# Another order of issue for a fused delta-rule attention and softplus MLP

## The chip, the cores and the metric

The kernel runs on one core of a Trainium2 chip. The metric is the device time of one execution in microseconds; lower is better. The core has a matrix engine (TensorE, PE in the profile, with the loading of its weights shown apart as PEld), three engines for elementwise work (VectorE = DVE, ScalarE = ACT, GpSimd = POOL) and SyncE (SP), which here only issues DMAs. Each of them works through a queue of its own in the order in which the instructions were written, and waits on semaphores for the others.

## The reference

Inputs are q, k, v and g of shape (4, 8, 768, 48), beta of shape (4, 8, 768), and two weights, `w_in` (384 x 2048) and `w_out` (2048 x 384). A gated delta rule runs over the 768 tokens, for 4 x 8 heads of width 48:

```python
k_n = k / (np.linalg.norm(k, axis=-1, keepdims=True) + 1e-06)
for t in range(S):
    readout = np.einsum('bhd,bhde->bhe', q[:, :, t], state)
    y[:, :, t] = g[:, :, t] * readout
    v_old = np.einsum('bhde,bhd->bhe', state, kt)
    state = state + bt[:, :, :, None] * np.einsum('bhd,bhe->bhde', kt, vt - v_old)
```

Its output, seen as 3072 tokens of 384 features, goes through an MLP: `h = x @ w_in`, then softplus, `max(h, 0) + log1p(exp(-|h|))`, then `@ w_out`. The output is 3072 x 384 in float32.

## The kernel before, in words

**Tiling.** The 768 tokens are cut into 12 chunks of 64. A chunk has 64 tokens of each of 4 x 8 heads, that is 256 tokens of the MLP. Within a chunk the recurrence over tokens is written as a triangular system. Its matrix is made from products of the normalized keys, and inverted by block elimination. What one chunk hands to the next is the state alone, 48 x 48 for each head.

**Stages.** For each chunk there are these steps, and their names are used below:

- *Norms*: the keys are squared, summed (`red`, L413), and a root is taken: on ScalarE for the first four chunks, on GpSimd as a power for the others (L427). Two small VectorE steps follow (L435, L437).
- *Front*: keys and queries are cast or scaled to 16 bits (`kn` L509, `qn`), transposed by TensorE against an identity matrix (L461, L526) and copied out of PSUM (`kqt`, L222 on ScalarE and L224 on the other two). The keys of chunks 8 to 11 and the queries of chunks 10 and 11 are turned by transposing DMAs instead (L444). Gram products follow (L598), with scaled copies of them (`kk`, L222 or L226) and masked ones (`mt`, L580).
- *Inverse*, for the groups of chunks 0, 1, (2, 3), (4, 5), ... (10, 11): 15 elimination steps, each a product and a sum (L717, L724; the first is L709), which stand on VectorE or GpSimd; then copies and small matmuls which make `td` and `z`.
- *Chain*, the part that is serial from chunk to chunk: products with the old state (L914), w (L947 for chunk 0, L953 for the others), u1 and u2 (L967, L980), the state's product (`smm`, L996) and its sum (`s`, L1010), the output's product (L1022) and the gate (`yg`, L1036, two instructions for a chunk). The output is turned by transposing DMAs for chunks 5 to 10 (L1046), and by TensorE (L1062) with a copy (`xt`) for the others.
- *Dense*, the MLP: `w_in` products (`h`, L1088), softplus (`ga`, L1100), `w_out` products (`o`, L1115), a copy out of PSUM (`osb`) and the stores (L1139). Chunks 0, 1, 10 and 11 have windows of their own, and the others go in pairs.

**What sets the order.** Every step of every chunk is an item with a number: `Program.add` records what it does, which engines may do it and what it depends on. Nothing runs in the order in which the items are recorded. A table of words in text, `_ORDER`, lists them: the letter is the engine (P, D, A, G, S for PE, VectorE, ScalarE, GpSimd, SyncE), the number the item's, and `Program.emit` issues them word by word. An item may only stand behind all that it depends on. The place in the table thus sets the order in each engine's queue, and the letter the engine where an item allows several. Buffers come from rings, such as 12 slots for f32 inputs (`r_f`), 5 PSUM banks (`p_d`) for attention, 2 (`p_h`) for h and 1 (`p_o`) for o. An item's buffer takes the first free slot when its first user is issued, and gives it back with its last, so the order in the table also decides which slot a tile gets and whom it waits for:

```python
for word in table.split():
    en, no = word[0], int(word[1:])
    it = self.items[no]
    for b in it.bufs:
        if b.ap is None:
            b.slot = b.ring.free.pop(0)
    it.fn(en)
```

The weights come by DMA from GpSimd's queue, `w_in` and `w_out` in four pieces each, and all else from SyncE's. Ninety-six items are "fills": one matmul of the identity with itself, 128 x 512, into a slot of `h` that nobody reads. The table decides how many of them are issued:

```python
def fill(en, hp=hp):
    nc.tensor.matmul(hp.ap, ident, ident[:, None, :].broadcast_to([P, 4, P]))
```

Of the kernel before, what the change touches and what calls it, by code (L numbers as in the profile page):

```python
# [1170 lines left out]
G0 D6 S22 D329 S23 D267 P213 D13 A234 A1 D16 S31 D14 P18 D19 D241 P242 G238 D235 S17 S33 P239  # L1171
A243 P255 A236 D240 D237 D264 P252 A256 A257 A253 A254 D265 D266 G268 D269 D270 S32 D9 G308 S25
A8 D271 D272 A311 D273 D274 A7 S40 D275 G276 G277 G278 P20 P312 A4 A15 G279 S41 S24 A304 A2 A313
A12 A21 P309 A310 P314 P317 D244 G280 A10 P245 D305 S34 S50 G281 D5 D318 S49 A319 A11 A3 G282
A306 G283 A316 A248 D315 D307 A366 D327 P249 P220 A250 P224 A251 G131 G284 D326 D328 A391 A247
S51 S52 P323 P207 D330 P159 G331 D367 G332 A368 D392 P320 S27 S43 A246 D324 G333 P186 A377 D369
D322 A288 D285 A393 P378 A290 P228 D394 P261 P173 A289 P146 D325 A380 A286 D321 G334 D291 D263
A379 P295 A287 G395 G370 D262 S26 G335 P258 D292 A296 S42 A297 D260 P396 P163 D259 G130 D294
D336 G337 P209 D397 A293 S59 G410 A373 P298 A299 P371 S58 G338 G339 D372 D809 G411 A300 P374
A376 G133 P301 D810 A302 P168 P403 A375 D404 A303 D406 A405 P811 P398 P175 D812 D340 S29 S28 S30  # L1180
P139 A813 A456 P814 D402 A400 G132 D407 A816 D815 D457 D401 G341 A808 G342 P386 P820 S61 D399
A387 D821 A388 G343 P381 D822 G134 D344 P823 P196 G345 A382 D824 D383 G346 P1027 D389 D408 D390
A351 G458 G135 D385 A349 D409 S60 A463 D352 A1028 D412 A347 G136 P1021 D413 A1022 D384 A350 D414
G415 D353 P1023 G416 P464 A348 D354 D459 G417 S70 A1024 P1025 P817 A818 P1033 S35 S36 P357 G418
S69 A819 A1026 D358 D460 P826 D825 A465 A359 D356 G419 A355 P1035 P461 A1034 G137 G420 P1029
D828 D827 P360 D467 A1036 P1044 A362 A462 P829 D361 D421 A1030 P1031 D422 P830 A832 D423 D466
G424 A1032 D831 P1045 D425 G426 S68 P363 S67 A364 P468 D365 P833 P1046 A481 G427 P1047 D469 A834
D835 P476 A1048 A477 D482 S38 G428 P839 S39 S37 A470 D431 D480 A478 D479 S45 A429 P1037 D840
D841 P471 P836 A473 P1038 A432 D433 P842 P1039 G590 D837 D838 G483 A430 A843 D475 D434 D484 P844
A472 P438 A439 A440 D436 P1040 P1053 A437 S44 S77 G500 D845 P447 S76 G485 A1054 D474 P441 P1061  # L1190
A442 D435 D846 P486 S86 G546 A443 P848 A449 A448 D487 P1057 A850 S85 A1062 P444 P493 G501 A571
S47 D547 D446 A445 A849 P1065 D495 P847 A1058 D497 D496 P851 A852 G548 P1051 D494 A1066 A1041
D572 D853 G573 P488 D492 S46 S78 A489 A1052 D490 D549 P1055 D498 D499 G502 P450 S48 P1059 A1056
G503 P857 A452 G504 G505 A451 S79 A1060 G506 P854 G507 D491 D855 G508 G509 G510 G511 P1067 S104
G512 S53 S87 S54 P1063 P1068 D856 D859 D574 P862 P1069 A1064 P453 S88 A553 D864 A557 D863 P866
D858 D867 A454 D575 P1070 A868 S103 A455 P865 P869 A1071 P558 A660 A871 A559 S55 S56 P1074 S57
# [76 lines left out]
```

## Time and profile before

| | |
|---|---|
| median of 3 runs | 239.28 us (238.65 to 243.46) |
| profiled execution | 239.09 us |
| its span | 237.3 us |
| mean granted TensorE clock | 0.984 |
| PE busy | 206.0 us (87%) |
| VectorE, ScalarE, GpSimd busy | 162.8, 155.8, 115.3 us |
| DMA | 30.30 MB, mean 128 GB/s |

All times in the profile are of one profiled execution. The span is what lies between its first and last instruction, and 1.8 us of its 239.09 lie around the span. In rows that group instructions there stand the line, the engine, the operation, the output and inputs by name, their shapes and a count; behind the first bar the busy time in us and the mean of one in ns; behind the second the time for which the engine was idle just before them, with the instruction whose end ended that. PE's busy time counts pipelined matmuls and runs from the start of the first to the modelled end of the last, so it tells of work at hand and not of peak speed.

### The profile page before, as it was taken

To read this page: it belongs to the slowest core of one execution; us is meant where nothing else is said; L and a number is where in the kernel's file an instruction comes from. 1 tells how busy PE (TensorE), PEld (TensorE's weight loads), DVE (VectorE), ACT (ScalarE), POOL (GpSimd) and SP (SyncE) were. 2 spreads that over 40 slices of the span, in tenths; PEclk is the share of its full clock that TensorE was granted. 3 is DMA by queue.
4 is the path that set the end of the run, shared out by engine and by line. 5 is a ranking of instruction groups with operands and counts; after the bars stand their busy time and mean duration, and the time that the engine had idled before them with its cause. 6 is when DMAs were issued, how large, how long until landed. Compare 5 with 4: busy or idle time off the path is not lost.

```text
span 237.3 us, 11021 instructions
## 1 busy us (share of the span) xinstructions
PE 206.0 (87%) x4787; PEld 130.4 (55%) x4787; DVE 162.8 (69%) x371; ACT 155.8 (66%) x332; POOL 115.3 (49%) x223
## 2 busy tenths in 40 slices
PE   4837865977987999989599999889999999999992
PEld 3723543754665665556355556455555555667761
DVE  7898994989978899995689768966648043521000
ACT  4999893955886789957189886348663766035520
POOL 5248989576767888988864763104721000000000
PEclk9999995999999999999999999999999999999999
DMA  6999999999899188789399676888635301242222
GB/s 117 179 196 171 194 205 210 185 146 188 151 181 149 37 150 153 204 134 151 86 162 154 119 143 77 130 174 155 116 89 115 69 7 33 64 92 50 53 50 66
DMA packets 101136, 30.30 MB, mean 128 GB/s; under 512 B 91808, under 2 KB 101056, under 8 KB 101088
## 3 DMA queue, kind: packets, MB, share of 16 engines
q1 hardware_dynamic: 96128, 24.96, 61.6%
q0 software_dynamic: 3712, 3.15, 9.3%
q10 hardware_dynamic: 1248, 1.49, 2.6%
q8 instruction: 37, 0.61, 1.1%
q14 instruction: 11, 0.09, 0.2%
HBM read 25.26 MB, written 4.72 MB: 126 GB/s over the span
## 4 chain that ended last, share of the span: by engine, by line
PE 63%; DVE 9%; issue 6%; ACT 6%; POOL 6%; DMA 5%; SPq 3%; DVEq 0%; ACTq 0%; POOLq 0%
PE h L1088 22%; PE o L1115 20%; PE d L598 3%; PE d L914 3%; PE d L1115 2%; SPq L345 2%; POOL tt L724 2%; DMA kqt<-kn 2%; POOL tmp L717 2%; PE d L1022 2%; DMA f<-in_k_dram 2%; ACT kk L222 2%; DMA f<-in_g_dram 2%; PE d L980 1%; DVE mt L580 1%
## 5 line engine op out<-in xcount | busy, mean ns | idle before, releaser
L1088 PE MATMUL h<-xt,w_in 128*128 128x512 f16 (+1 forms) x384 | 74.0, 330 | 0.3 <-DVE xt L224 0.2
L1100 ACT ACTIVATE ga<-h 128x512 f16<-128x512 f32 x96 | 56.5, 601 | 26.1 <-PE h L1088 21.2
L1115 PE MATMUL o<-w_out,ga 128*128 128x384 f16 x352 | 66.1, 327 | 0.0
L1115 PEld LDWEIGHTS <-ga 128*128 128x128 f16 x384 | 35.1, 98 | 22.3
L1088 PEld LDWEIGHTS <-w_in 128*128 128x128 f16 x384 | 35.1, 99 | 20.9 <-issue 0.7
L717 POOL TENSOR_TENSOR tmp<-nn,tt 128x56 f32<-128x56 f32 (+13 forms) x78 | 29.6, 379 | 19.9 <-DVE tt L724 12.1
L724 POOL TENSOR_TENSOR tt<-tt,tmp 128x56 f32<-128x56 f32 (+13 forms) x78 | 29.0, 372 | 6.1
L222 ACT ACTIVATE osb<-o 128x384 f32<-128x384 f32 x17 | 8.4, 492 | 25.1 <-PE o L1115 20.8
L427 POOL TENSOR_TENSOR nv<-nv,half_c 128x16 f32<-128x16 f32 x8 | 23.5, 2937 | 2.0 <-DVE nv L413 1.8
L580 DVE TENSOR_TENSOR mt<-d,mask 128x256 f16<-128x256 f32 x48 | 18.6, 410 | 4.8 <-ACT kk L222 2.2
L598 PE MATMUL d<-kqt 48*64 48x128 f16 (+1 forms) x448 | 11.4, 228 | 8.1 <-ACT kqt L222 4.6
L224 DVE CAST u<-d 128x384 f16<-128x384 f32 x21 | 11.4, 552 | 10.1 <-PE d L967 5.5
L1036 DVE TENSOR_TENSOR yg<-d,f 128x384 f16<-128x384 f32 x24 | 12.5, 546 | 8.4 <-ACT ga L1100 4.5
L222 ACT ACTIVATE u<-d 128x384 f16<-128x384 f32 x27 | 12.8, 494 | 6.0 <-PE d L980 3.2
L598 PEld LDWEIGHTS <-kqt 48*64 48x64 f16 x448 | 8.1, 118 | 14.8 <-issue 8.6
L222 ACT ACTIVATE kqt<-d 128x512 f16<-128x512 f16 (+1 forms) x23 | 14.1, 636 | 1.8 <-DVE w L953 0.8
L222 ACT ACTIVATE kk<-d 128x256 f16<-128x256 f32 x33 | 11.8, 385 | 4.9 <-PE d L598 3.1
L1010 DVE TENSOR_TENSOR s<-s,d 128x384 f16<-128x384 f16 x20 | 10.3, 542 | 5.8 <-PE d L996 5.4
L953 DVE TENSOR_TENSOR w<-f,d 128x384 f16<-128x384 f32 x22 | 11.5, 547 | 2.8 <-PE d L914 1.6
L413 DVE TENSOR_REDUCE nv<-f 128x16 f32<-128x768 f32 x12 | 11.2, 942 | 0.5 <-ACT f L402 0.5
L914 PEld LDWEIGHTS <-kqt 48*64 48x64 f16 x704 | 7.8, 108 | 6.2 <-issue 6.2
L914 PE MATMUL d<-s,kqt 48*64 48x48 f16 x704 | 9.7, 188 | 0.8 <-DVE qn L224 0.5
(134 smaller groups left out, 334.4 us busy)
## 6 DMA issues: line engine op xcount, KB each, us to landing
f<-in_k_dram SPq DMA_DIRECT2D x24, 192.0 KB, 7.5
f<-in_q_dram SPq DMA_DIRECT2D x24, 192.0 KB, 4.9
f<-in_v_dram SPq DMA_DIRECT2D x24, 192.0 KB, 4.7
out_dram<-osb SPq DMA_DIRECT2D x33, 96.0 KB, 3.4
f<-in_g_dram SPq DMA_DIRECT2D x24, 96.0 KB, 3.4
f<-in_g_dram SPq DMA_DIRECT2D x12, 192.0 KB, 5.6
w_in<-in_moe_w_in_dram POOLq DMA_DIRECT2D x4, 384.0 KB, 7.6
w_out<-in_moe_w_out_dram POOLq DMA_DIRECT2D x4, 384.0 KB, 8.9
```

The source lines that it names most:

```text
L222: nc.scalar.activation(o, x, AF.Copy, scale=float(sign))
L427: nc.gpsimd.tensor_tensor(nvs(), nvs(), half_c[:, :NU], ALU.pow)
L580: nc.vector.tensor_tensor(mt[c][p].ap[:, NP * g : NP * g + NP], bank(gb, p, n), mask[:, None, :].broadcast_to([P, NP, C]), ALU.mult)
L598: nc.tensor.matmul(o, kq(c, r, NP * g + i, FEAT[p], 0, C), x)
L717: ENG[en].tensor_tensor(t, nn.ap[:, :nb, j : j + 1, j + 1 :].broadcast_to([P, nb, w, n]), tt.ap[:, :nb, :w, j : j + 1].broadcast_to([P, nb ...
L724: ENG[en].tensor_tensor(rows, rows, t, ALU.add)
L914: nc.tensor.matmul(where(r, p)[:, h], kq(c, r, h, FEAT[p], off, off + C), s0[r].ap[FEAT[p], h], **start(h),)
L953: lambda en, p=p: nc.vector.tensor_tensor(w1[p].ap, vf.ap[:, p], hd(wp[p].ap), ALU.subtract),
L1036: lambda en, a=a: nc.vector.tensor_tensor(yg.ap[:, a], hd(yp[a].ap), gf.ap[:, a], ALU.mult),
L1088: nc.tensor.matmul(hp.ap[:, n * b : n * b + n], w_in[:, j, f * P : (f + 1) * P], xt.ap[:, j, t0 : t0 + n], start=(j == 0), stop=(j == 2),)
L1100: lambda en, hp=hp, o=gb: nc.scalar.activation(o.ap, hp.ap, AF.Softplus),
L1115: nc.tensor.matmul(op.ap[:, :DM], b.ap[:, col + c0 : col + c0 + 128], w_out[:, f, :], start=(f == 0), stop=(f == NF - 1),)
```

## The change

Only the table changes: `Program`, all items and their functions are the same letter for letter. The new table lists the same items in another order, and without the fifteen fills that the old one issues at its beginning. It has 1286 words where the old one has 1301. Of the 1286 items that both have, 212 stand on another engine: 60 go from ScalarE to VectorE and 56 from VectorE to ScalarE, 30 from VectorE to GpSimd and 29 back, 9 from ScalarE to GpSimd and 2 back; 14 DMAs go from SyncE's queue to ScalarE's and 12 back. The items per engine go from 320 to 323 on VectorE, from 327 to 318 on ScalarE, from 126 to 134 on GpSimd and from 160 to 158 on SyncE. The pieces of the weights come in another order: `w_in` pieces 1, 0, 3, 2 and then `w_out` 0 to 3 before; `w_in` 2, 3, 1, `w_out` 2, 1, 0, `w_in` 0, `w_out` 3 now. Each line of the table differs; the diff's first and last lines show the kind:

```diff
 _ORDER = """
-G0 D6 S22 D329 S23 D267 P213 D13 A234 A1 D16 S31 D14 P18 D19 D241 P242 G238 D235 S17 S33 P239
-A243 P255 A236 D240 D237 D264 P252 A256 A257 A253 A254 D265 D266 G268 D269 D270 S32 D9 G308 S25
...
+P1370 A1342 S1343 D1372 A1371 A1373 S1374
 """
```

What this makes of the queues is seen at three places. In these rows a name's number is that of the buffer.

VectorE up to chunk 0's gate (`yg`, L1036). `mt` are masked Gram products of later chunks, `kk` scaled ones, `tmp` and `tt` an elimination step, `nv` sums of squared keys, `u` chunk 0's. Before:

```order
L580 TENSOR_TENSOR mt_112<-d_176,mask 128x256
L224 CAST u_138<-d_174 128x384
L717 TENSOR_TENSOR tmp_120<-nn_118,tt_121 128x63
L724 TENSOR_TENSOR tt_121<-tt_121,tmp_120 128x9x7
L580 TENSOR_TENSOR mt_113<-d_176,mask 128x256
L580 TENSOR_TENSOR mt_113<-d_172,mask 128x256
L224 CAST u_141<-d_174 128x384
L413 TENSOR_REDUCE nv_98<-f_81 128x16
L580 TENSOR_TENSOR mt_112<-d_173,mask 128x256
L226 TENSOR_SCALAR kk_103<-d_173 128x4x64
L1036 TENSOR_TENSOR yg_148<-d_175,f_79 128x384
L1036 TENSOR_TENSOR yg_148<-d_174,f_79 128x384
```

The same place in the changed kernel:

```order
L724 TENSOR_TENSOR tt_121<-tt_121,tmp_120 128x12x4
L580 TENSOR_TENSOR mt_111<-d_176,mask 128x256
L717 TENSOR_TENSOR tmp_120<-nn_118,tt_121 128x39
L724 TENSOR_TENSOR tt_121<-tt_121,tmp_120 128x13x3
L717 TENSOR_TENSOR tmp_120<-nn_118,tt_121 128x28
L724 TENSOR_TENSOR tt_121<-tt_121,tmp_120 128x14x2
L413 TENSOR_REDUCE nv_97<-f_83 128x16
L580 TENSOR_TENSOR mt_110<-d_173,mask 128x256
L1036 TENSOR_TENSOR yg_148<-d_174,f_78 128x384
L717 TENSOR_TENSOR tmp_120<-nn_118,tt_121 128x15
L724 TENSOR_TENSOR tt_121<-tt_121,tmp_120 128x15
L1036 TENSOR_TENSOR yg_148<-d_175,f_78 128x384
```

Seven elimination steps of chunk 1 (steps 6 and 7 and the last five) now stand on VectorE ahead of chunk 0's second `yg`, and the last of them between its two; the copies of u stand on ScalarE or farther ahead. From chunk 0's first w (L947) to its second `yg` there are 15 rows in between before and 31 now.

SyncE around the transposing DMA of chunk 11's keys (`kqt`, L444). The gates g come in three pieces, one of L345 and two of L337; `f_78` holds chunk 8's gate, `f_82` chunk 9's, and the rows with `out_0_dram` are stores. Before:

```order
L444 DMA_TRANSPOSE kqt2_106<-kn3_92 128x8x128
L337 DMA f1_78<-in_g_dram 64x8x48
L1139 DMA out_0_dram<-osb0_168 64x384 x2
L345 DMA f1_78<-in_g_dram 64x16x48
L1139 DMA out_0_dram<-osb2_170 64x384
L345 DMA f5_82<-in_g_dram 64x16x48
L1139 DMA out_0_dram<-osb2_170 64x384
L337 DMA f5_82<-in_g_dram 64x8x48
L345 DMA f4_81<-in_v_dram 64x16x48 x2
L345 DMA f7_84<-in_v_dram 64x16x48
L337 DMA f5_82<-in_g_dram 64x8x48
L337 DMA f1_78<-in_g_dram 64x8x48
```

In the changed kernel the keys of chunk 10 are the second row and those of chunk 11 the sixth, `xt` is the output of chunks 6 and 7 as the MLP reads it, and chunk 8's gate is in slot `f_84`:

```order
L444 DMA_TRANSPOSE kqt2_106<-qn1_94 128x8x128
L444 DMA_TRANSPOSE kqt2_106<-kn3_92 128x8x128
L1046 DMA_TRANSPOSE xt1_151<-yg0_148 128x3x128
L1139 DMA out_0_dram<-osb2_170 64x384
L444 DMA_TRANSPOSE kqt3_107<-qn0_93 128x8x128
L444 DMA_TRANSPOSE kqt3_107<-kn2_91 128x8x128
L1139 DMA out_0_dram<-osb2_170 64x384
L1046 DMA_TRANSPOSE xt1_151<-yg1_149 128x3x128 x2
L1046 DMA_TRANSPOSE xt1_151<-yg0_148 128x3x128
L345 DMA f7_84<-in_g_dram 64x16x48
L345 DMA f4_81<-in_v_dram 64x16x48 x2
L345 DMA f6_83<-in_v_dram 64x16x48
```

One piece of chunk 8's gate still stands behind the key transposes, and its two others stand ahead of all four of them; the outputs of chunks 6 and 7 are now turned among them.

PE's first rows, as a difference (L287 makes beta, L526 transposes keys):

```order
-L1268 UNCONDITIONAL_BRANCH
-L1149 LDWEIGHTS ident
-L1149 MATMUL h_177<-ident 128x512
+L1267 UNCONDITIONAL_BRANCH
 L287 MATMUL d_172<-w_out 128x32 x4
 L526 LDWEIGHTS kn_89
```

The fills at the start of the queue are gone; PE has 9546 rows before and 9516 now.

More of the change, by code (lines that the diff above doesn't have):

```diff
@@ L1177 @@
[L1177 to L1182, printed above, removed]
@@ L1243 @@
+P1355 A1356 P1353 P1327 A1354 A1328 A1304 P1367 S1305 P1357 A1358 P1361 S1306 P1375 A1362 P1365
+S1320 P1323 A1324 P1376 P1377 P1368 A1366 P1329 P1331 A1330 P1378 P1337 P1333 D1379 S1299 A1380
+P1344 A1334 P1345 P1338 A1332 S1381 P1346 P1347 P1339 P1340 S1312 D1341 A1348 A1350 S1349 P1369
+P1370 A1342 S1343 D1372 A1371 A1373 S1374
 """
```

131 lines of the change are left out of this document (67 added, 64 removed).

## The prediction

> **What bounds the kernel now.** I read the page's totals first, then busy time by stretch, then the waits of VectorE, then the chain.
>
> ```profile
> span 237.3 us, 11021 instructions
> PE 206.0 (87%) x4787; PEld 130.4 (55%) x4787; DVE 162.8 (69%) x371; ACT 155.8 (66%) x332; POOL 115.3 (49%) x223
> PEclk9999995999999999999999999999999999999999
> ```
>
> No single engine fills the span, so the stretches decide. Columns: the stretch, its length, then busy time (and count) of PE, weight loads, DVE, ACT, POOL, then granted clock, DMA share and GB/s.
>
> ```profile
> 0.00:40.00 40.00, 25.20 (x485) 17.23 (x486) 33.61 (x106) 32.63 (x71) 26.75 (x67) 0.94 1.15 181
> 40.00:80.00 40.00, 33.83 (x945) 24.17 (x945) 35.36 (x74) 28.23 (x63) 28.24 (x43) 0.97 1.07 161
> 80.00:100.00 20.00, 19.98 (x551) 12.13 (x549) 19.25 (x37) 18.49 (x40) 17.88 (x30) 1.00 0.71 141
> 100.00:120.00 20.00, 15.99 (x490) 10.16 (x488) 14.80 (x30) 10.35 (x23) 17.19 (x35) 1.00 0.77 129
> 120.00:145.00 25.00, 25.00 (x668) 13.79 (x665) 19.56 (x47) 20.93 (x46) 13.67 (x26) 1.00 0.79 138
> 145.00:170.00 25.00, 22.91 (x571) 13.05 (x570) 18.95 (x40) 14.15 (x32) 8.25 (x17) 1.00 0.83 142
> 170.00:220.00 50.00, 50.00 (x994) 30.82 (x993) 19.84 (x40) 26.03 (x54) 3.32 (x10) 1.00 0.29 64
> 220.00:237.30 17.30, 13.14 (x95) 9.05 (x93) 1.47 (x3) 5.03 (x10) 0.00 (x0) 0.98 0.24 58
> ```
>
> PE is idle for 14.80 + 6.17 = 21.0 us in the first 80 us, for 4.0 us from 100 to 120, for 2.1 us from 145 to 170, and for 4.2 us at the very end, behind the last matmul. Elsewhere it has no gap: from 80 us on the kernel is bound by PE with two leaks, 6.1 us together. Ahead of 80 us VectorE is the fullest engine, 33.61 + 35.36 = 69.0 of 80 us, and it hardly waits. Its largest two waits between 6 and 80 us (engine, what waited, for whom; us, times, longest) are these:
>
> ```profile
> DVE xt L224 <- PE d L1062: 2.9, 1, 2.9
> DVE tmp L717 <- POOL tt L724: 1.0, 1, 1.0
> ```
>
> So the early stretch is a VectorE queue in order, fed just in time. The chain names the leaks (start, length, what):
>
> ```profile
> 36.62 2.11 issue
> ...
> 105.32 0.96 issue
> ...
> 113.10 2.56 issue
> ...
> 150.77 4.28 DMA kqt<-kn
> ...
> 162.92 3.73 DMA f<-in_g_dram
> ```
>
> "issue" is PE standing still inside a run of matmuls while it waits for nothing that the profile shows: 2.11 us in the transposes of chunk 0's y (which is also the 2.9 us above), 0.96 and 2.56 us in the leak from 100 to 120. The leak from 145 to 170 is SyncE's: the transposing DMA of chunk 11's keys, and then chunk 8's gate, which lands late.
>
> **The change part by part.** PE's matmuls are the same but for the fills, so a gain can only come out of the 31 idle microseconds, and a loss only adds to them.
>
> *VectorE up to chunk 0's y.* Between its first w (L947) and its second yg (L1036) VectorE has 15 rows before and 31 now. The prices (columns: group, count; busy, mean ns; idle before it and whose end ended that):
>
> ```profile
> L580 DVE TENSOR_TENSOR mt<-d,mask 128x256 f16<-128x256 f32 x48 | 18.6, 410 | 4.8 <-ACT kk L222 2.2 <-PE d L598 1.6 <-ACT ta L738 0.9
> L724 DVE TENSOR_TENSOR tt<-tt,tmp 128x39 f32<-128x39 f32 (+13 forms) x20 | 4.8, 239 | 0.7
> L717 DVE TENSOR_TENSOR tmp<-nn,tt 128x39 f32<-128x39 f32 (+13 forms) x20 | 4.7, 236 | 3.1 <-POOL tt L724 2.8
> L509 DVE TENSOR_TENSOR kn<-f,nv 128x768 f16<-128x768 f32 x5 | 5.0, 993 | 0.0
> L224 DVE CAST z<-d 128x256 f16<-128x256 f32 x11 | 4.4, 418 | 6.5 <-PE d L877 6.5
> L437 DVE RECIPROCAL nv<-nv 128x16 f32<-128x16 f32 x10 | 2.4, 237 | 0.1
> L435 DVE TENSOR_SCALAR nv<-nv 128x32 f32<-128x32 f32 (+1 forms) x4 | 0.8, 212 | 0.0
> L690 DVE COPY tt<-beta_p 128x32 f32<-128x32 f32 x2 | 0.7, 356 | 0.0
> L226 DVE TENSOR_SCALAR kk<-d 128x256 f16<-128x256 f32 x15 | 6.1, 411 | 0.6 <-PE d L598 0.5
> L224 DVE CAST u<-d 128x384 f16<-128x384 f32 x21 | 11.4, 552 | 10.1 <-PE d L967 5.5 <-PE d L980 4.4
> L224 DVE COPY kqt<-d 128x1024 f16<-128x1024 f16 (+1 forms) x7 | 4.5, 647 | 0.8 <-PE d L526 0.8
> ```
>
> Added: six elimination steps of two instructions (6 x 0.475 = 2.85), two masks (0.82), the norms' two small ones (0.45), a diagonal (0.36), one key scaling (0.99), two z (0.84): 6.31. Removed: two L226 (0.82) and two u (1.10): 1.92. Net 4.4 us. Ahead of that w the changed queue is shorter: four masks (1.64) and two steps (0.95) fewer, one copy of kqt more (0.65), the small rest about even: 1.9 less. Together +2.5 us for the second yg; instructions overlap a little, but VectorE has no wait there that could absorb it. Bounds: 0, if the ordering ends waits on PE that these rows stand beside, and 4.4, if the shorter head only waits for data. Between chunk 0's y and chunk 1's state product (L996) the changed order has less VectorE work (99 items ahead of that product, 104 before), between chunks 1 and 2 more (139 against 129), so I carry about +3 us to 80 us, with bounds 0 and 4.4; from there PE hands it on.
>
> *The leaks after 100 us.* In the changed SyncE queue the gate loads g8 stand, but for one piece, ahead of the key transposes of chunks 8 to 11; the loads of k, q, v, g for chunks 4 to 9 stand far ahead of their readers, where before several stood next to them. The 2.1 us from 145 to 170 goes. Of the 4.0 us from 100 to 120, 0.96 + 2.56 = 3.5 us is "issue", which no row ties to a queue that moves; I let it stay and take 0.5 us. Gain 2.6 us; bounds 0 (a later transfer is late instead) and 6.1.
>
> *The fills.* Fifteen matmuls whose product nobody reads go:
>
> ```profile
> L1149 PE MATMUL h<-ident 128*128 128x512 f16 x15 | 6.9, 520 | 3.0 <-DVE ident L206 3.0
> ...
> 23.05 1.06 PE L461 MATMUL d<-ident,qn 128*128 128x128 f16 x8
> ...
> 26.24 0.61 PE L526 MATMUL d<-ident,kn 128*128 128x128 f16 x8
> ```
>
> Their 6.9 us lie in PE's idle time, so nothing is gained but what stood in someone's way, 0 to 1 us. What they may buy is the clock: eight transposes take 1.06 us at 23 us and 0.61 us at 26 us. Without fills the three groups of transposes between 26 and 36 us could cost 0.45 us more each, 1.35 us, and the first matmuls of dense work at half speed a little more; VectorE's queue covers most of it. Cost 0.5 us, bounds -1 and +3. [...]
>
> *What moves between engines.* 212 of 1286 items change their engine; the counts per engine hardly change (VectorE 320 to 323, ScalarE 327 to 318, GpSimd 126 to 134). Which of them count is in the term above; from 170 us on neither engine matters, since PE is busy for 50.00 of 50 us.
>
> Sum: +3.0 - 2.6 + 0.5 = +0.9 us on a span of 237.3. The profiled execution took 239.09 us, 1.8 us around its span and 0.2 below the median of 239.28. Forecast 240 us.
>
> **The rivals.** *Faster: both leaks close and the early cost is hidden.* The wait of 2.9 us behind chunk 0's y need not recur, and with transfers issued early the "issue" stops, which fall where DMA is crowded (share 1.15 in the first 40 us, 0.77 from 100 to 120), may go with them. For it: after 80 us PE has always work when data is there. Against: nothing shows what "issue" waits for. Time: 239.1 - 6.1 = 233.0, and 231 if the 2.11 us goes too.
>
> *Slower: GpSimd's added work holds VectorE up.* Up to chunk 4's state product GpSimd takes on three more casts, four more tx copies, chunk 1's scaling of v and several clears, all beside the fullest engine.
>
> ```profile
> 29.85 1.12 DVE L947 TENSOR_TENSOR w<-f,nv 128x384 f16<-128x384 f32 x2
> 30.00 0.56 POOL L717 TENSOR_TENSOR tmp<-nn,tt 128x63 f32<-128x63 f32 x1
> 31.22 0.31 POOL L717 TENSOR_TENSOR tmp<-nn,tt 128x64 f32<-128x64 f32 x1
> L509 POOL TENSOR_TENSOR kn<-f,nv 128x768 f16<-128x768 f32 x5 | 7.4, 1484 | 4.6 <-PE d L996 3.4 <-DVE nv L437 1.2
> ```
>
> A GpSimd step of 0.31 us took 0.56 us beside a VectorE instruction that reads two SBUF tensors. If the stall goes the other way too, four full-size GpSimd instructions (1.484 us each, 5.9 us) stand against VectorE, and they come on top of the 4.4 us bound: 239.1 + 4.4 + 5.9 - 2.6 = 246.8 at worst; with half of the 5.9 us, 243.9. It decides once VectorE is busy for over 73 of the first 80 us instead of 69. Against it: before, GpSimd was busy for 55 of those 80 us without a wait of VectorE on it beyond 1.0 us. [...]
>
> *The change does nothing here.* If PE's total sets the end, only its idle time counts, and the new order closes one leak where it opens another: 238 to 240. That is the forecast's own middle.
>
> **How the numbers follow.** Forecast (small terms that cancel): 0.50. Faster rival: 0.26. Slower rival: 0.24. Some 2% of 239.3 us is what the runs shown can tell from no change (they spread from 238.65 to 243.46), so faster means below 234.5 and slower above 244.1. The forecast's own range from its terms: all at their good end 239.1 + 0 - 6.1 - 1 = 232.0, all at their bad end 239.1 + 4.4 + 3 = 246.5; half of each side, 235.5 to 243, holds most of it. The range to give has the faster rival in it and the slower one at its worst nearly: 232 to 246.5. The faster rival's 0.26 lies below 234.5 nearly whole, and the forecast's lower end adds 0.02: 0.28. Of the slower rival's 0.24 half lies above 244.1, and the forecast's upper end, where the clock or a new wait costs all of its bound, adds 0.10: 0.22. Within 2%: 0.50.
>
> **What would show it.** VectorE runs chunk 0's two yg back to back:
>
> ```profile
> 35.17 1.01 DVE L1036 TENSOR_TENSOR yg<-d,f 128x384 f16<-128x384 f32 x2
> ```
>
> They end at 36.2 us now; right if the second ends at 37 to 41. Leaks: PE's idle time from 145 to 170 us falls under 1 us, and the chain no longer holds a wait on in_g there; wrong if a DMA of a y (L1046) or a v replaces it. Fills: eight transposes (L461, L526) still at over 1 us after 26 us, and PE at full clock by 50 us. Faster rival: no "issue" piece over 1 us. Slower rival: VectorE instructions between SBUF tensors (L717, L947, L1010) with longer means than now. The forecast is wrong as a whole if PE's idle time in the first 80 us moves by over 5 us either way.

## The result and the profile after

The changed kernel takes 249.07 us (median of 4 runs, 248.34 to 250.93) beside 238.97 us for the kernel before on the same chip (4 runs, 237.76 to 243.46): a ratio of 1.045, 95% interval 1.037 to 1.054. It is slower, and its time lies above the range given. Ratios leave disturbed runs out, so they can differ a little from the quotient of two medians. The profiled execution took 248.88 us with a span of 247.2, 9.9 us more than before.

The page's totals of the changed kernel:

```profile
span 247.2 us, 11000 instructions
PE 208.1 (84%) x4772; PEld 133.1 (54%) x4772; DVE 166.1 (67%) x381; ACT 152.6 (62%) x319; POOL 119.7 (48%) x224
```

Busy time by stretch of the changed kernel, with the stretches and columns of the prediction:

```profile
0.00:40.00 40.00, 20.45 (x384) 16.35 (x385) 34.53 (x104) 25.36 (x51) 27.88 (x68) 1.00 1.14 179
40.00:80.00 40.00, 31.63 (x882) 22.25 (x884) 33.16 (x77) 27.43 (x59) 29.72 (x39) 0.96 1.08 180
80.00:100.00 20.00, 17.19 (x489) 11.66 (x477) 17.05 (x32) 12.91 (x24) 12.24 (x28) 1.00 0.61 116
100.00:120.00 20.00, 18.09 (x512) 10.22 (x512) 16.78 (x34) 15.32 (x36) 15.92 (x23) 1.00 0.71 111
120.00:145.00 25.00, 23.74 (x586) 13.82 (x584) 19.59 (x46) 19.17 (x45) 17.66 (x30) 1.00 0.81 146
145.00:170.00 25.00, 24.25 (x634) 14.00 (x633) 20.60 (x42) 14.30 (x33) 8.42 (x19) 1.00 0.72 108
170.00:220.00 50.00, 49.87 (x1144) 28.53 (x1142) 22.36 (x47) 27.64 (x57) 7.91 (x21) 1.00 0.36 73
220.00:247.20 27.20, 22.89 (x172) 16.28 (x169) 2.03 (x4) 10.45 (x20) 0.00 (x0) 0.98 0.20 51
```

The table is best read from its end. PE's busy time still to come is 156.0 us at 80 us, where it was 147.0 before: 9.0 us behind. Counted in this way the changed kernel is 11.8 us behind at 100 us, and 9.7 at 120. Ahead of 80 us this count misleads, since the same matmul counts for more at a lower granted clock: from 75.6 to 79.0 us, where that is 0.50, four products of L1115 take 1.46 us (at 76.23), and four take 0.82 at 50.53 in the kernel before, where it is 1.00. Over the whole span PE is busy for 208.1 us now and, without the time of the fills alone, for 200.8 before, with the same 4772 matmuls. An estimate that gives each matmul still to come the mean time that its line and shape take in the kernel before behind 110 us (of the faster half where none runs so late) puts the changed kernel 1.4 us behind at 40 us, 3.5 at 50, 7.0 at 80 and 10.5 at 100. From 120 us on PE's idle time sums to 6.5 us in one kernel and 6.2 in the other. So the 10 us build up between 40 and some 100 us, and the two leaks that the prediction looked at no longer matter: from 145 to 170 us the idle time went from 2.09 to 0.75, and from 100 to 120 from 4.01 to 1.91. In their place 80 to 100 us, which had no gap (0.02), now has 2.81.

**Where the first part goes: chunk 0's y.** VectorE in the changed kernel (start, length, what; at the end idle time before it and who ended that):

```profile
8.62 1.39 DVE L631 COPY_PREDICATED nl<-mb,nl 128x16 uint32<-128x16 uint32 x1
...
24.12 0.44 DVE L740 TENSOR_SCALAR ta<-tt,mx 128x256 f16<-128x256 f32 x1 [0.87 <-POOL tt L724]
...
31.11 0.55 DVE L947 TENSOR_TENSOR w<-f,nv 128x384 f16<-128x384 f32 x1
...
36.61 0.68 DVE L717 TENSOR_TENSOR tmp<-nn,tt 128x55 f32<-128x55 f32 x1 [0.35 <-POOL tt L724]
...
41.29 0.56 DVE L1036 TENSOR_TENSOR yg<-d,f 128x384 f16<-128x384 f32 x1 [0.66 <-ACT kk L222]
...
42.08 0.56 DVE L1036 TENSOR_TENSOR yg<-d,f 128x384 f16<-128x384 f32 x1
```

The second `yg` ends at 42.64 us; before it ended at 36.18, so it is 6.5 us late (in a second profile of the changed kernel, taken below, it ends at 41.66 and is 5.5 us late). The queue is late from its start on. Its first w begins at 31.11, before at 29.85: 1.3 us later. From there to the second `yg`'s end go 11.5 us, before 6.3. The changed kernel up to that w and from it to y's end, in the columns of above, where the third busy time is VectorE's:

```profile
0.00:31.11 31.11, 14.99 (x216) 12.30 (x216) 26.45 (x79) 18.32 (x37) 21.02 (x56) 1.00 1.11 173
31.11:42.64 11.53, 6.99 (x228) 5.17 (x220) 10.03 (x33) 8.62 (x19) 9.11 (x13) 1.00 1.26 204
```

The same two stretches of the kernel before:

```profile
0.00:29.85 29.85, 19.41 (x315) 13.65 (x315) 26.49 (x87) 24.84 (x55) 17.63 (x48) 1.00 1.12 172
29.85:36.18 6.33, 4.23 (x185) 2.82 (x171) 6.28 (x17) 5.77 (x13) 5.68 (x15) 0.93 1.28 202
```

Up to the w VectorE has eight instructions fewer but the same busy time, and it is idle for 4.7 us instead of 3.4. From the w on it is busy for 3.8 us more and idle for 1.5 us more. The first row of VectorE's above is one cause of this: the small copy took 0.18 us before, and now 1.39, beside the squaring of chunk 1's keys that now stands on GpSimd.

VectorE's same row in the kernel before:

```profile
8.40 0.18 DVE L631 COPY_PREDICATED nl<-mb,nl 128x16 uint32<-128x16 uint32 x1
```

GpSimd at that time in the changed kernel:

```profile
8.51 1.47 POOL L404 TENSOR_TENSOR f<-f 128x768 f32<-128x768 f32 x1 [0.70 <-DMA f<-in_k_dram]
```

PE in the changed kernel, from the transposes after 26 us to chunk 0's first dense product (L1088), and a later group of transposes:

```profile
27.79 1.03 PE L526 MATMUL d<-ident,kn 128*128 128x128 f16 x8 [1.87 <-POOL kn L509]
...
38.33 0.37 PE L526 MATMUL d<-ident,kn 128*128 128x128 f16 x2 [1.29 <-issue]
...
40.19 0.20 PE L1022 MATMUL d<-u,mt 64*64 64x48 f16 x1 [0.94 <-ACT u L222]
...
41.90 0.26 PE L598 MATMUL d<-kqt 48*64 48x128 f16 x1 [0.26 <-DVE yg L1036]
42.69 0.64 PE L598 MATMUL d<-kqt 48*64 48x128 f16 x15 [0.53 <-DVE yg L1036]
...
45.54 0.82 PE L1088 MATMUL h<-xt,w_in 128*128 128x256 f16 x3
...
61.50 0.61 PE L461 MATMUL d<-ident,qn 128*128 128x128 f16 x8 [0.94 <-ACT kqt L222]
```

The same product L1088 began at 40.07 before. PE waits here for all three others in turn: for GpSimd's key scaling, inside a run of transposes for nothing shown, for ScalarE's u (which stands behind a copy of `kqt` there), and then for both `yg`.

**Where the second part goes: two readers of one PSUM tile.** The masked copy `mt` (L580, VectorE) and the scaled copy `kk` (L222, ScalarE) read the same Gram tile in PSUM, and the one that stands second in the program waits for the first, here for up to 3.16 us. The waits view of the kernel before (who waits, for whom: us, times, longest):

```profile
DVE mt L580 <- ACT kk L222: 2.2, 2, 1.9
...
ACT kk L222 <- DVE mt L580: 1.3, 2, 0.8
```

The same view of the changed kernel:

```profile
ACT kk L222 <- DVE mt L580: 5.4, 4, 3.2
...
DVE mt L580 <- ACT kk L222: 4.8, 6, 2.7
```

3.5 us of such waits have become 10.2. The longest one ends at 100.31 us. VectorE there, in the changed kernel:

```profile
98.93 0.96 DVE L740 TENSOR_SCALAR ta<-tt,mx 128x256 f16<-128x256 f32 x1 [0.37 <-POOL tt L724]
99.81 1.07 DVE L580 TENSOR_TENSOR mt<-d,mask 128x256 f16<-128x256 f32 x3
```

ScalarE at the same time:

```profile
100.31 0.38 ACT L222 ACTIVATE kk<-d 128x256 f16<-128x256 f32 x1 [3.16 <-DVE mt L580]
100.59 0.48 ACT L222 ACTIVATE osb<-o 128x384 f32<-128x384 f32 x1
```

And PE:

```profile
101.13 2.11 PE L1115 MATMUL o<-w_out,ga 128*128 128x384 f16 x12 [1.82 <-ACT osb L222]
```

VectorE's mask stands in its queue behind `ta`, which waits for GpSimd's last elimination step; ScalarE's `kk` waits 3.16 us for that mask; `osb`, behind `kk` in ScalarE's queue, empties the only PSUM bank of `o`; and PE waits 1.82 us for it, from 99.3 on, which is 0.7 of the new gap between 80 and 100 us. (1.75 of it is a stop inside a run of matmuls, shown in the last section.) The waits stand in both directions, 5.4 and 4.8 us; why one reader waits for the other no run shows.

### The profile page after: what moved, and what is told of

Same layout as the page of the kernel before. It is cut to its first block, busy times and chain, and to the rows that moved or that the text cites. A ratio compares the mean times of both kernels' runs of the same rounds, so it can differ in the third digit from the quotient of the medians.

```text
span 247.2 us, 11000 instructions
## 1 busy us (share of the span) xinstructions
PE 208.1 (84%) x4772; PEld 133.1 (54%) x4772; DVE 166.1 (67%) x381; ACT 152.6 (62%) x319; POOL 119.7 (48%) x224
## 4 chain that ended last, share of the span: by engine, by line
PE 59%; DVE 17%; ACT 8%; issue 6%; POOL 6%; DMA 2%; SPq 0%; DVEq 0%; ACTq 0%; POOLq 0%
PE h L1088 22%; PE o L1115 20%; PE d L914 3%; POOL tt L724 3%; POOL tmp L717 3%; PE d L1115 2%; DVE mt L580 2%; ACT kk L222 2%; DMA f<-in_k_dram 2%; ACT ga L1100 2%; PE d L598 2%; PE d L877 2%; PE d L980 1%; DVE nv L413 1%; PE d L824 1%
## 5 line engine op out<-in xcount | busy, mean ns | idle before, releaser
L1088 PE MATMUL h<-xt,w_in 128*128 128x512 f16 (+1 forms) x384 | 75.0, 332 | 0.4 <-issue 0.3
L1115 PE MATMUL o<-w_out,ga 128*128 128x384 f16 x352 | 66.2, 328 | 2.8 <-ACT osb L222 1.8
L1115 PEld LDWEIGHTS <-ga 128*128 128x128 f16 x384 | 35.8, 98 | 25.6 <-issue 3.4
L1088 PEld LDWEIGHTS <-w_in 128*128 128x128 f16 x384 | 34.7, 99 | 20.1 <-issue 0.9
L717 POOL TENSOR_TENSOR tmp<-nn,tt 128x126 f32<-128x126 f32 (+11 forms) x71 | 28.5, 401 | 17.3 <-DVE tt L724 8.5
L724 POOL TENSOR_TENSOR tt<-tt,tmp 128x126 f32<-128x126 f32 (+11 forms) x71 | 26.1, 368 | 5.6
L580 DVE TENSOR_TENSOR mt<-d,mask 128x256 f16<-128x256 f32 x48 | 18.4, 410 | 5.7 <-ACT kk L222 4.8
L598 PE MATMUL d<-kqt 48*64 48x128 f16 (+1 forms) x448 | 13.9, 243 | 9.1 <-ACT kqt L222 4.4
L222 ACT ACTIVATE osb<-o 128x384 f32<-128x384 f32 x19 | 9.3, 490 | 18.9 <-PE o L1115 18.8
L222 ACT ACTIVATE kqt<-d 128x512 f16<-128x512 f16 (+1 forms) x24 | 15.1, 672 | 5.5 <-PE d L526 3.9
L222 ACT ACTIVATE kk<-d 128x256 f16<-128x256 f32 x39 | 13.5, 391 | 7.9 <-DVE mt L580 5.4
L598 PEld LDWEIGHTS <-kqt 48*64 48x64 f16 x448 | 9.3, 126 | 14.2 <-issue 6.2
L1036 DVE TENSOR_TENSOR yg<-d,f 128x384 f16<-128x384 f32 x24 | 12.6, 550 | 4.8 <-PE d L1022 3.1
L222 ACT ACTIVATE u<-d 128x384 f16<-128x384 f32 x27 | 12.7, 494 | 4.0 <-PE d L967 2.1
L526 PE MATMUL d<-ident,kn 128*128 128x128 f16 x64 | 6.9, 264 | 6.7 <-POOL kn L509 1.9
L914 PEld LDWEIGHTS <-kqt 48*64 48x64 f16 x704 | 7.6, 109 | 7.9 <-issue 7.8
L839 ACT ACTIVATE xs<-d,mk 128x128 f16<-128x128 f32 x26 | 7.9, 369 | 5.8 <-PE d L824 5.6
```

Of the source, the lines that this page charges most:

```text
L222: nc.scalar.activation(o, x, AF.Copy, scale=float(sign))
L580: nc.vector.tensor_tensor(mt[c][p].ap[:, NP * g : NP * g + NP], bank(gb, p, n), mask[:, None, :].broadcast_to([P, NP, C]), ALU.mult)
L598: nc.tensor.matmul(o, kq(c, r, NP * g + i, FEAT[p], 0, C), x)
L717: ENG[en].tensor_tensor(t, nn.ap[:, :nb, j : j + 1, j + 1 :].broadcast_to([P, nb, w, n]), tt.ap[:, :nb, :w, j : j + 1].broadcast_to([P, nb ...
L724: ENG[en].tensor_tensor(rows, rows, t, ALU.add)
L914: nc.tensor.matmul(where(r, p)[:, h], kq(c, r, h, FEAT[p], off, off + C), s0[r].ap[FEAT[p], h], **start(h),)
```

## The experiments

The theory at first: chunk 0's y is late, and its lateness is handed to the end. The rivals: the fills' absence (eight transposes in 1.03 us instead of 0.61), GpSimd's work beside VectorE's, and waits that lie later in the order. Words of the table are quoted with the engine's letter and the item's number, and its rows are cut to the words around an edit.

**The fills, both ways.** The changed kernel with fifteen fills put into PE's queue in its first 26 us, and the kernel before without its fifteen:

```diff
-G3 G241 P18 G5 G6
+G3 G241 P213 P18 G5 G6
...
-A9 P312 D266 G269
+A9 P312 P220 P224 D266 G269
...
```

```diff
-G0 D6 S22 D329 S23 D267 P213 D13 A234 A1
+G0 D6 S22 D329 S23 D267 D13 A234 A1
...
```

> The changed order with the fifteen unread matmuls put back between 3 and 32 us (one at the start, the others into TensorE's waits up to chunk 0's inverse). Clock theory (without fills TensorE runs at half speed until 48 us, and that is most of the 10 us): eight transposes take 0.61 instead of 1.05 us at 28 us, time falls by 4 us or more, to 245 or less. Order theory (the loss is the order in which the queues stand, and the slow clock only goes with it): within 1.5 us of the changed kernel, 247.5 to 250.5.

> The kernel before, without its fifteen unread matmuls and otherwise word for word. Clock theory: TensorE stays at half speed until its first run of dense work, chunk 0's serial products each take twice as long, 242 us or more. Order theory: 238 to 240.5. The forecast's own term for the fills was +0.5 us, with bounds -1 and +3.

> The kernel before without its fifteen unread matmuls once more, in five rounds: 0.97 to 0.99 of the kernel before if the first result holds (they then cost time themselves), 0.99 to 1.01 if it was chance.

With fills the changed kernel took 249.82 us (ratio to before 1.033, 1.025 to 1.042), no better than without, and the second `yg` still ended at 42.95. But there the fills did not speed PE up: its granted clock was 0.82 in the first 40 us, and the transposes took as long as without them. So this run doesn't tell what a faster PE would be worth to the changed kernel. PE of it:

```profile
27.77 1.04 PE L526 MATMUL d<-ident,kn 128*128 128x128 f16 x8 [0.47 <-POOL kn L509]
```

Without fills the kernel before took 238.74 (0.982, 0.973 to 0.991), and in more rounds 241.48 (1.014, 1.002 to 1.026; the medians of all runs there are 241.48 and 241.78). The two signs differ, so in the old order the fills are worth nothing that these runs can tell. PE of the kernel without fills, second run: the transposes are slow, chunk 0's second `yg` ends at 37.04, 0.9 us late, and the dense products start 1.4 us earlier than the 40.07 of before all the same, since the stop of 2.11 us ("issue") is not in this run.

```profile
28.38 1.04 PE L526 MATMUL d<-ident,kn 128*128 128x128 f16 x8
...
38.67 3.83 PE L1088 MATMUL h<-xt,w_in 128*128 128x256 f16 x18 [0.65 <-DVE xt L224]
```

**Head and rest exchanged.** The words up to 40 us from one table, and all that is left in the order of the other. First the old head (235 words) with the new rest, then the new head (238 words) with the old rest:

```diff
-G0 G329 S22 S23 G3 G241 P18 G5 G6 A14 D11 D8 D238
...
+G0 D6 S22 D329 S23 D267 P213 D13 A234 A1 D16 S31
...
+D824 D383 G346 S35 S69 G136 S70
```

```diff
-G0 D6 S22 D329 S23 D267 P213 D13 A234 A1 D16 S31
...
+G0 G329 S22 S23 G3 G241 P18 G5 G6 A14 D11 D8 D238
...
+D349 A824 D13 A7 A12 P320
```

> The first 235 words of the old table (up to chunk 0's xt, about 40 us of the kernel before, fills included), then all that is left in the changed table's order. Head theory (what is lost before 40 us is handed on to the end): it gains back all but 2 us, 239 to 242. Middle theory (the order between 40 and 105 us leaves TensorE idle, by 8 of the 10 us): 245 to 249.

> The first 238 words of the changed table (up to chunk 0's state product, about 45 us), no fills, then all that is left in the old table's order. Head theory: 246 to 249. Middle theory: 240 to 243, about the 2 us by which TensorE's remaining work lags at 40 us.

Both are slow: 248.43 us (1.033, 1.025 to 1.041) and 249.85 (1.034, 1.024 to 1.045). But the seam makes waits that neither kernel has, since the heads load the weights' pieces in another order than the rests need them. PE of the old head with the new rest:

```profile
43.26 2.74 PE L1088 MATMUL h<-xt,w_in 128*128 128x256 f16 x12 [3.57 <-DMA w_in<-in_moe_w_in_dram]
```

PE of the new head with the old rest:

```profile
52.29 2.74 PE L1088 MATMUL h<-xt,w_in 128*128 128x256 f16 x12 [6.59 <-DMA w_in<-in_moe_w_in_dram]
```

So the same two again, with the weights' pieces in the order of the rest:

```diff
-P249 P220 A250 P224 A251 G131 G284
+P249 P220 A250 P224 A251 G132 G284
...
```

```diff
-D285 A377 D21 G132 D394 P261 P258
+D285 A377 D21 G131 D394 P261 P258
...
```

> As with the old head (first 235 words of the old table, then the rest in the changed order), but the eight pieces of the weights in the order that the changed table's first dense work wants them (w_in 2, 3, 1 first). In the old-head run TensorE stood 3.6 us for w_in piece 2, which the old head loads last: an artefact of the cut. Without it: 244 to 246 if head (2 us at 40 us) and middle (the rest) each lose their share; 239 to 242 if the head alone was the loss.

> As with the new head (first 238 words of the changed table, then the rest in the old order), but the weights in the old order, since TensorE stood 6.6 us for w_in piece 0 there. 241 to 244 if the new head costs only the 2 to 4 us by which it lags at 50 us; 247 or more if the order of the head spoils what comes after it, whatever the rest's order.

The new head with the old rest takes 246.61 us (1.025, 1.017 to 1.034), that is 6.0 us more than before, and no wait for a weight is left in it: its second `yg` ends at 41.70, 5.5 us late. So the new head, with its seam, costs a good half of the loss. The old head with the new rest, where the second `yg` ends at 36.20 as before, takes 249.80 (1.036, 1.025 to 1.048), which the theory did not allow. There PE is held later. Its stretch from 40 to 60 us, with the columns of the other stretches:

```profile
40.00:60.00 20.00, 16.30 (x375) 11.38 (x370) 16.07 (x35) 8.49 (x17) 17.19 (x28) 0.60 1.16 183
```

PE is busy for 16.30 of the 20 us, at a granted clock of 0.60, and ScalarE for 8.49, where it was 13.28 before. The rest of the new order does not serve an early y: softplus stands on ScalarE behind a copy for chunk 1 whose data isn't there yet. ScalarE of the same run:

```profile
45.95 0.41 ACT L222 ACTIVATE tx<-td 64x256 f16<-64x256 f16 x1 [3.48 <-DVE td L787]
```

How much of this run's loss is that wait and how much the granted clock of 0.60, no run separates.

**Later seams.** The old order up to 60 us (352 words) and up to 105 us (636 words), then the rest in the new order:

```diff
-G0 G329 S22 S23 G3 G241 P18 G5 G6 A14 D11 D8 D238
...
+A429 P1037 D840 D841 S78 S76 S44
...
```

```diff
-G0 G329 S22 S23 G3 G241 P18 G5 G6 A14 D11 D8 D238
...
+A536 A885 A886 P1083 G646 S74 A1049
...
```

> The first 352 words of the old table (up to 60 us of the kernel before; all weights are loaded in them), then the rest in the changed order. If the changed order loses as much between 60 and 105 us as TensorE's idle time in the changed kernel says (5 to 6 us more than before): 244 to 246. If the loss is all before 60 us: 239 to 241.

> The first 636 words of the old table (up to 105 us of the kernel before), then the rest in the changed order. If the changed order behind 105 us costs nothing, as TensorE's idle time says (it even closes the leak at 145 to 170 us, 2.1 us, of which my forecast made its gain): 237 to 240. If it loses there too: 242 or more.

They take 246.32 us (1.035, 1.025 to 1.045) and 249.05 (1.044, 1.029 to 1.059). Each loses its time at its seam: the first between 60 and 80 us, where PE is busy for 14.38 of 20 us (17.42 before), the second in one wait. PE of the second:

```profile
112.78 0.63 PE L980 MATMUL d<-u,z 64*64 64x48 f16 x31 [7.10 <-ACT td L222]
```

ScalarE stands there behind the squaring of chunk 10's keys, whose load the new order issues early and the old one had not issued yet. These two runs tell of seams, and of the new order only this: from some 130 us on it loses nothing, since the second loses nothing behind its wait.

**GpSimd.** The new order with the old engine for each of the items that changed theirs; and the new order with only the squaring of chunk 1's keys back on ScalarE:

```diff
-G0 G329 S22 S23 G3 G241 P18 G5 G6 A14 D11 D8 D238
+G0 D329 S22 S23 A3 D241 P18 D5 D6 D14 A11 A8 G238
...
```

```diff
-S50 S34 G267 S41 G304 A234 P239 A19
+S50 S34 G267 S41 A304 A234 P239 A19
```

> The changed order with the old engine for each of the 212 items that changed theirs. Engine theory (GpSimd's added casts and the swaps between ScalarE and VectorE make the loss): 244.5 or less. Order theory (it is who stands behind whom in a queue, whichever queue): 247 or more, or slower still, since the order was made for the new engines.

> The changed kernel with one letter changed: the squares of chunk 1's keys (L404 on GpSimd at 8.51 us, 1.47 us) go back to ScalarE. In the changed kernel VectorE's L631 took 1.39 us beside them instead of 0.18 and chunk 0's inverse starts 2.5 us late. [...]

With the old engines it is 264.68 us (1.102, 1.092 to 1.112): PE is busy for 17.31 of the first 40 us, 25.20 before (fills included) and 20.45 after. The new order does not suit the old engines. With the one item back, 249.83 us (1.038, 1.029 to 1.047), VectorE's small copy took 0.18 us again, so GpSimd's squaring was what stretched it. But it started 3.2 us later, since ScalarE's queue now has chunk 1's squaring ahead of chunk 0's, and waits for chunk 1's keys (3.85 us before both, in its row). The stall is real and of 1.2 us; what it costs at the end this run does not tell.

VectorE with the one item back:

```profile
11.84 0.18 DVE L631 COPY_PREDICATED nl<-mb,nl 128x16 uint32<-128x16 uint32 x1
```

ScalarE of the same kernel:

```profile
8.51 1.58 ACT L402 ACTIVATE f<-f 128x768 f32<-128x768 f32 x2 [3.85 <-DMA f<-in_k_dram]
```

**The pairs of readers.** Three words of the changed table moved, so that ScalarE's copy of two tiles (items 478 and 563) stands ahead of VectorE's masks of them, and one mask (479) ahead of a copy:

```diff
-P1037 D480 A478 A487 G548 S94 S57 P848 A451 A452 G646 P471 A1052 S95 G573 A477 S104 A473 D479
+P1037 A478 D480 A487 G548 S94 S57 P848 A451 A452 G646 P471 A1052 S95 G573 D479 A477 S104 A473
...
-A1088 D882 D577 D521 D565 D564 P1099 P1083 A563
+A1088 D882 D577 D521 A563 D565 D564 P1099 P1083
```

> The changed kernel with three words moved, on the same engines: the reading of a Gram tile by ScalarE (kk, L222) now stands ahead of VectorE's reading of the same tile (mt, L580) for tiles 4.11 and 6.01, and VectorE's ahead of ScalarE's for 4.10. In the changed kernel the second reader waited for the first: ScalarE 1.72 us at 72.2 and 3.16 us at 100.3, VectorE 2.68 us at 74.9, though the tiles were ready; TensorE stood 0.43 + 0.73 us at 72 and 1.82 us at 99 behind them, and its clock was at half from 75.6 to 79.0. Pair theory: these waits go, and the time falls by 3 to 4.5 us, to 244.5 to 246. If another wait stands right behind them: 248 to 250.

It takes 246.56 us, between what the two theories had and 2.5 less than the changed kernel's 249.07, which was measured on another chip (ratio to before 1.036, 1.020 to 1.051). The waits of this kernel:

```profile
DVE mt L580 <- ACT kk L222: 3.0, 5, 1.4
...
ACT kk L222 <- DVE mt L580: 0.5, 2, 0.2
```

10.2 us of waits have become 3.5 again, and the 1.82 us of PE at 101 us is gone: the same twelve products run from 97.99 us on, behind no wait.

**The head mended by hand.** A few words of the changed table moved before 42 us: the squaring of chunk 1's keys to ScalarE, behind the work for chunk 0; two copies of queries and a mask behind the transpose of chunk 0's inverse (L779); a copy of keys behind u2; a group of key transposes behind chunk 0's u2 product (L980); and VectorE's last elimination step behind the second `yg`. First these alone, then with the three words of above, then with five more words of chunk 1's and 4's work; and on the same chip the changed kernel as it is:

```diff
-S50 S34 G267 S41 G304 A234 P239 A19
+S50 S34 G267 S41 A234 P239 A19
...
-D256 A254 D265 A9 P312 D266 G269
+D256 A254 D265 A304 A9 P312 D266 G269
...
-A400 A456 G2 P814 S76 A372 D457 A815 D402 A816 S44 S39 P820 D821 D346 D822 G134 G458 P386 S56
+S68 A400 A456 G2 S76 D457 A815 D402 A816 A372 S44 S39 P820 D821 D822 D346 G134 G458 P386 S56
```

> The changed kernel with eight words moved ahead of 42 us: chunk 1's key squares go to ScalarE behind chunk 0's scaled keys (no GpSimd stall of L631), two copies of kqt and a mask stand behind chunk 0's st instead of ahead of it on VectorE, chunk 0's last copies of u (u2) ahead of chunk 2's kqt on ScalarE with their product (L980) ahead of chunk 2's transposes on TensorE, and chunk 0's second yg ahead of chunk 1's last elimination step. Carry theory (the late head is handed on): second yg ends at 38 to 40 us instead of 42.6, and the time falls by 3 us or more against the changed kernel. Swallowed (the next wait is chunk 1's inverse, which does not start from that y): yg comes earlier, the time falls by 1 us or less.

> The head of e13 and the three words of e9 together. If the two add: 5 us or more below the changed kernel. If the head is swallowed: about 2.5 us below it, as e9.

> e14, and on ScalarE chunk 4's kqt and q copies ahead of two softplus that wait (TensorE stood 0.94 + 0.62 us for them at 61 us), on VectorE chunk 1's transpose st ahead of chunk 2's ln (1.95 us). If the loss is a sum of such waits: 2 us below e14. If each opens the next: as e14, or slower.

> The changed kernel as it is, as the base of the other three on the same chip: 1.037 to 1.054 of the kernel before, as measured first.

The changed kernel took 248.53 us again (247.38 to 249.48; 1.041, 1.035 to 1.047). The mended head took 247.90 (1.037, 1.030 to 1.043), the head with the pairs 246.49 (245.23 to 247.61; 1.031, 1.024 to 1.038), and with the five words more 246.01 (245.10 to 247.21; 1.030, 1.024 to 1.036). On this chip, then, the head gives 0.6 us, the pairs 1.4 more, and the last five words 0.5. The runs overlap, so the pairs' price is only known roughly, as some 1.4 to 2.5 us. The head's words hardly moved y, which fits with the little that they gave. VectorE of the mended head:

```profile
40.26 1.02 DVE L1036 TENSOR_TENSOR yg<-d,f 128x384 f16<-128x384 f32 x2 [0.77 <-ACT kk L222]
```

It ends at 41.28; in the second profile of the changed kernel it ended at 41.66. From the first w (29.96) to there VectorE is still busy for 9.7 of 11.3 us: nearly all of the work that was moved ahead of y still stands there.

**What a late y costs.** In the kernel before, the two instructions of chunk 0's y are issued seven times over (the repeats write the same values), and nothing else is changed:

```diff
-                  lambda en, a=a: nc.vector.tensor_tensor(
-                      yg.ap[:, a], hd(yp[a].ap), gf.ap[:, a], ALU.mult),
+                  lambda en, a=a: [nc.vector.tensor_tensor(
+                      yg.ap[:, a], hd(yp[a].ap), gf.ap[:, a], ALU.mult)
+                      for _ in range(7 if c == 0 else 1)],
```

> The kernel before, with chunk 0's two yg (L1036) written seven times each instead of once: twelve instructions more on VectorE at 36 us, 0.48 to 0.55 us each, so that chunk 0's y ends 5.8 to 6.6 us later, as in the changed kernel, and all of VectorE's queue behind it too. Carry theory: 244.5 to 246 (5 us or more above before, measured beside it). Swallowed: 1 us above it or less. In between: the share that the head has in the 10 us.

VectorE of this kernel:

```profile
35.19 8.12 DVE L1036 TENSOR_TENSOR yg<-d,f 128x384 f16<-128x384 f32 x14
```

It ends at 43.31, 7.1 us late. The median is 246.41 us beside 240.56, and the ratio 1.023 (1.015 to 1.030), that is 5.5 us (3.6 to 7.3). So about three quarters of such a lateness reach the end, and between half and all of it by the interval. By the estimate of above, PE's work in this run is 3.6 us behind at 50 us, 5.3 at 80 and 7.3 at 100, a course like that of the changed kernel. Two things make the price rough: the repeats are work added to VectorE's queue, where the changed kernel only moves work ahead, and PE's granted clock from 40 to 60 us is 0.76 here and 0.95 in the kernel before.

**The gate alone.** In the kernel before, chunk 8's gate loads were moved behind the transposing DMA of chunk 6's second output piece, and chunk 11's keys' ahead of chunk 7's, which is the one part of the change that the forecast's gain rests on:

```diff
-D690 D935 P938 G691 S729 S933 A1156
+D690 D935 P938 G691 S729 S933 S100 S102 S101 A1156
...
-P732 A699 A1184 S951 A733
+P732 A699 A1184 A733
...
-A700 G746 P1196 P1197 D946 S950
+A700 G746 S747 S951 S950 P1196 P1197 D946
...
```

> The kernel before with six words of SyncE's moved: chunk 8's three gate loads ahead of the transposes around 144 us, and the transposing DMA of chunk 11's keys ahead of the two of chunk 7's output. The forecast's gain (2.1 us of TensorE's idle time from 145 to 170): 1.5 to 2.5 us below the kernel before. If the transposes only change places (chunk 7's output then comes late for the dense work of 6 and 7): 0 to 0.5 us.

It took 243.37 us (240.90 to 247.37; 1.011, 1.002 to 1.020), a little more than before. PE of the kernel before, and its wait for the keys:

```profile
155.09 0.64 PE L598 MATMUL d<-kqt 48*64 48x128 f16 x32 [1.77 <-DMA kqt<-kn]
```

PE of this kernel, where that wait is gone and another stands at its place:

```profile
154.65 1.46 PE L1088 MATMUL h<-xt,w_in 128*128 128x512 f16 x3 [3.27 <-DMA xt<-yg]
```

The transposes of chunk 7's output now come behind the gate and the keys, and PE's dense products wait for them. Within one queue a leak can be handed around; that it closes in the changed kernel takes more than these words.

## Why the prediction was wrong

**VectorE's queue up to chunk 0's y** was the right place, and its term the one mis-sized: +2.5 us (bounds 0 to 4.4) against 6.5, or 5.5 in the second profile, both beyond the bounds. The step that failed first is the head's gain. The prediction counted 1.9 us less work ahead of the first w, and so an earlier start; the w starts 1.3 us later, which makes 3.2 of the 4.0 us that are missing. VectorE's busy time up to it did not fall (26.45 us, 26.49 before), with 1.2 us of it in the stretched copy, and its idle time grew by 1.3 us: it also waits for others, 0.87 us each for chunk 0's keys and for GpSimd's last elimination step. From that w to the second `yg` the prediction expected 4.4 us more, and 5.2 came: 3.8 us are busy time, so the moved steps were priced nearly right, and the rest are waits, for GpSimd's steps and ScalarE's `kk`, that it had left out.

**Handing on.** "I carry about +3" was for a y 2.5 us late. With 6.5 us and the three quarters of the late-y run, an estimate gives some 5 us (3.3 to 6.7) of the loss of 10 from here, and 4.2 with the 5.5 us of the second profile. The new head with the old rest, 6 us at 5.5 late, fits.

**"From there PE hands it on"** failed as a step. It held that between 80 and 100 us, where PE had no gap, none would come. 2.81 us came: 1.75 of "issue" and 0.7 of the wait for `osb` are the most of it. "What moves between engines" was set to 0 by counting items per engine; what counts is which of two readers of a tile stands first, and what stands ahead of it on its engine. The three words moved show it for the waits, which go back to 3.5 us; the time went down by 1.4 and by 2.5 us in two comparisons whose runs overlap.

**"A loss only adds to" PE's idle time** failed as well. Of the 9.9 us by which the span grew, 7.4 us are longer busy time of the same 4772 matmuls, many of them of the long kind, as the eight transposes in 1.03 us. The kernel before without fills has as much busy time (208.6 us in its second profile, of 242.50 us), so longer matmuls alone need not cost that; what they cost in the changed kernel no run shows.

**The leaks** went as forecast or better: 145 to 170 us under 1 us (0.75), and 2.1 us less from 100 to 120, where 0.5 was taken. But a leak's end is a gain only where the stretch is bound by PE alone, and the gate run shows no gain from that part. The 3.5 us of "issue" at 105 and 113 us did end, and one of 1.75 us came at 82.7.

**The fills** cost nothing measurable in the old order (0.5 forecast); in the changed one their absence is not priced, since the fifteen put back did not make PE faster there (eight transposes in 1.04 us, granted clock 0.82 in the first 40 us). Their signs came as described: eight transposes take 1.03 us at 27.79, and 0.61 at 61.50; the long durations end at 48.3, since twelve products of L1088 take 2.74 us at 45.54 and six take 0.83 at 48.61. That the fills buy clock is not shown: the granted clock reads 1.00 in the first 40 us of the changed kernel and 0.94 with the fills before, so the long matmuls show in their durations alone. The upper bound of +3 us has 1.35 us from the transposes, and no run shows the rest; in its place the kernel before without fills gave ratios of 0.982 and 1.014.

**The tests named.** y at 37 to 41 was missed by 1.6 us (0.7 in the second profile). PE's idle time in the first 80 us moved by 7.0 us, which was to mean that the forecast is wrong as a whole; but the fills' 6.9 us had counted as busy there, so this test could not tell what it was meant to. The work left at 80 us would have been the better one.

**The rivals.** *Slower by GpSimd's added work:* its time, 243.9 to 246.8, was nearest, and its mechanism shows once, in the 1.39 us copy. Its price isn't this: L631 is 1.2 us, and giving the engines back made it slower by over 15 us. Its condition did not come either: VectorE is busy for 67.7 of the first 80 us, not over 73. *Faster:* the leaks did close, the early cost wasn't hidden, and two "issue" stops over 1 us are there (1.29 and 1.75). *Nothing:* no.

**What stays open.** 5 and 1.4 to 2.5 us leave some 3 us of the 10 that no run assigns, and the first of these is an estimate from the late-y run. The long matmuls up to some 48 us (eight transposes in 1.03 us) are a rival for part of it: no run of the new order had shorter ones there. Nor is shown what the rest of the new order costs with an early y: each exchange of head and rest adds a seam of its own, and the old head with the new rest is as slow as the whole. Moving y forward inside the changed kernel, the direct proof, failed twice. No version beat the kernel before: the one without fills was faster in one comparison and slower in the next.

## What to carry to other kernels

When an order of issue is changed on several in-order queues, don't sum the instructions of one queue: follow the serial chain (here to chunk 0's y) across the engines, with the waits on each handover, and then ask what share of a delay reaches the end. Look for tiles with two readers on different engines, and see what stands ahead of the first reader, since everything behind the second waits for that too (here 3.16 us on ScalarE, and 1.82 us on PE behind it). And to compare two orders, look at the work that is still to come at a given moment, counted at one speed, and don't expect much of splicing them: all six splices of head and rest here were slower than the kernel before.

## What the runs showed of the hardware that was not expected

A COPY_PREDICATED of 128x16 took 0.18 us or, beside a GpSimd product of 128x768 f32, 1.39 us: until GpSimd's instruction had ended (8.51 + 1.47 = 9.98, and 8.62 + 1.39 = 10.01).

PE's "issue" stops, which the prediction could not place, come behind a packet of the DMA queue that the profile calls "instruction". PE of the changed kernel:

```profile
82.34 0.39 PE L996 MATMUL d<-u,kn 64*64 64x48 f16 x26
84.47 0.24 PE L996 MATMUL d<-u,kn 64*64 64x48 f16 x6 [1.75 <-issue]
```

That queue from 81.8 to 83.1 us in the same profile (packets, MB, share of 16 engines):

```profile
q8 instruction: 1, 0.02, 6.0%
```

That one packet of 16 KB (the page has 37 of them with 0.61 MB) runs from 81.81 to 83.07, and PE goes on 1.4 us later. At all seven "issue" stops over 0.9 us in the two profiles (packets from 35.4, 81.8 and 123.1 after; 35.7, 69.5, 103.7 and 113.4 before) PE goes on 1.3 to 1.5 us behind the end of such a packet. Each profile has 37 of these packets, and most have no such stop behind them. That they are the cause is argued from this, and no run took them away: stops of 0.93 to 2.56 us stand behind seven of the 74.
